# Three layers on one core: more places for the streamed weight blocks, the last attention pairs three steps apart, another order of issue

## The chip, the cores and the metric

One Trainium2 chip; the program runs on one of its cores. Five engines work side by side, each in its own order: PE (TensorE, matrix products; its weight loads stand apart as PEld), DVE (VectorE), ACT (ScalarE), POOL (GpSimd) and SP (SyncE, which here only issues DMAs). The metric is device microseconds of one execution; lower is better.

## The reference

Three parts follow each other. The second and third take their input from the part before them.

```python
# q, k, v: (4, 8, 576, 64) float32
out_d = softmax(mean4(q) @ mean4(k).T / 8) @ mean4(v)       # sequence pooled by 4
out   = repeat(out_d, 4) + softmax_near(q @ k.T / 8) @ v    # near: |i - j| < 4
x = out as (2304, 512)
h = x @ w_in;  g = max(h, 0) + log1p(exp(-abs(h)));  x = g @ w_out   # first layer, 512 -> 2048 -> 512
h = x @ w_in2; g = h * cos(h);                       y = g @ w_out2  # second layer, same sizes
```

The weights arrive as float64. The products are made of 16-bit pieces: each operand is split in a high and a low part, and three matmuls (high by high, high by low, low by high) stand for one.

## The kernel before

**Tiles and products.** The 2304 tokens are five tiles: 0 to 3 of 512 tokens, 4 of 256. L1 and L2 are the first layer's two products, L3 and L4 the second layer's. Attention is 16 pairs of heads (batch b, column c). L1 and L2 keep their weights in on-chip memory (`w1i_t`, `w1o_t`). L3 and L4 use schemes with seven products in place of eight, so their weights grow to seven quarters.

**Second weights.** A block of `w2i` or `w2o` is loaded as float64, decoded on ACT and DVE (`rebase`, `top`, `join`, `bound`, four `sums`, `high`, `low`: class `Second`), and stored to device memory (`scr_in`, `scr_out`). `second(n)` adds the decodes of n blocks to the program; it is called beside the first layer's units. The decode uses room that attention has had (`place2`); the room of the decode becomes the places of the last stage (`place3`).

**Streamed blocks.** L3 reads `scr_in` once for each of the five tiles: 40 loads of 896 KB into two places, `ri0` and `ri1`. L4 reads `scr_out`: 7 products by 2 halves by 5 tiles, 70 loads of 512 KB into four places, `ro0` to `ro3`. A place is refilled when the last matmul that reads it is done. For tile 4 such a block serves 12 matmuls of 256 columns, for a longer tile 24. All loads stand in SP's queue, one behind the other.

**Who sets the order.** The code adds operations to a plan (`Plan.add`) with a cost on each engine that may do them. `due()` works out backward when each has to be done; `move()` adds offsets from the table `MOVES`; `order()` runs a list schedule forward in which a place is taken when free. What comes out is the order of each engine's instructions, and it is held to (each engine's instructions are tied to the one before). Work that either ACT or DVE may do (casts `gh`, splits `high`, `xhi`) goes to the one that is free there. PE takes its matmuls in this order and passes none over.

**Steps.** `step()` counts first-layer units on their way into the plan: 28 are counted before tile 1's first unit, and each unit of a later tile counts two. Attention pair 4 and later ones are added at the steps in `POS1`, `POS2`, `POS3`. While attention has little for PE, matmuls on a tile of zeros (line 2089) are put in.

Names that the prediction uses: line 1386 is L1's matmul, 1623 L2's, 1430 L3's, 1722 L4's; 1681 takes L4's sums out of PSUM; 531 and 533 are one cast on ACT and on DVE, 525 and 527 one scaling; `xt0` to `xt4` hold the inputs of the tiles, in L1 and again in L3.

Of the kernel before, what the change touches and what calls it, by code (L numbers as in the profile page):

```python
# [27 lines left out]
NB = NF // 2  # L28
# [25 lines left out]
POS2 = (37, 41, 45, 49)  # L54
POS3 = (54, 58, 62, 66)
# [6 lines left out]
ONES, FROM, LONG = range(0, 10, 2), (4, 0), (2, 4)  # L62
# [9 lines left out]
W2STEP = 2  # L72
# [103 lines left out]
class Op:  # L176
    def __init__(self, n, cost, fn, claim, name, table=""):
        self.n, self.cost, self.fn, self.claim, self.name, self.table = n, cost, fn, claim, name, table
        self.succ, self.wait, self.values = set(), 0, set()
        self.hook, self.key = None, ""  # L180
# [1993 lines left out]
```

## Time and profile before

| | us |
|---|---|
| median of 3 runs | 857.46 |
| the runs | 855.68, 857.46, 859.52 |
| the profiled execution | 859.96 |
| its span, first to last instruction | 858.1 |
| busy: PE, DVE, ACT | 822.7, 734.8, 543.5 |

The stretches: to about 100 us attention and the decode of the first weights; to about 300 the rest of attention beside tiles 0 to 2 of the first layer; to 470 tiles 2 to 4 beside the decode of the second weights; from 470 L3 and L4, with L3 of one tile beside L4 of the tile before it; from about 823 L4 of the last tile alone.

A busy PE in this profile may still be late: its matmuls overlap, so the spacing of their ends tells their pace. A wait is idle time of an engine that something else ended.

### The profile page before, as it was taken

Reading aid. Unit: us, or ns where it says so; the run is one execution under the profiler, and the core shown is the slowest. Engines: PE = TensorE matmul, PEld = TensorE weight load, DVE = VectorE, ACT = ScalarE, POOL = GpSimd, SP = SyncE. Lnnn points to the kernel's source line nnn. Section 1 sums busy time; section 2 is a strip of 40 time slices with the busy share of each in tenths; the row PEclk is TensorE's granted clock in tenths of the full one; section 3 lists DMA queues with packets and bytes.
Section 4 is the critical chain, followed back from the end, with each engine's and each line's share of the span. In section 5 each row is a group of like instructions: output and inputs, shape, how many; then the busy total and the mean of one; then the engine's idle time right before and its main releaser. Section 6 shows DMA issues by size and latency. Waiting matters only on the chain.

```text
span 858.1 us, 16959 instructions
## 1 busy us (share of the span) xinstructions
PE 822.7 (96%) x6837; PEld 543.3 (63%) x6837; DVE 734.8 (86%) x1570; ACT 543.5 (63%) x924; POOL 1.8 (0%) x9
## 2 busy tenths in 40 slices
PE   7988999999999999989999999999999999999986
PEld 3643555445555644434456888888666788888875
DVE  6999999866579867699999899999999999997651
ACT  3569999532244579799998789664565555564320
POOL 0000000000000000000000000000000000000000
PEclk9999999999999999999999999999999999999999
DMA  9887421202210054356746633356546576578676
GB/s 298 281 282 260 173 98 61 75 1 61 95 45 17 2 190 148 136 226 231 233 163 214 245 100 116 130 171 235 196 155 222 172 244 212 192 232 280 227 239 227
DMA packets 49310, 147.73 MB, mean 172 GB/s; under 512 B 3857, under 2 KB 22929, under 8 KB 45137
## 3 DMA queue, kind: packets, MB, share of 16 engines
q1 hardware_dynamic: 49232, 146.67, 50.9%
q8 instruction: 53, 0.87, 0.4%
q14 instruction: 25, 0.20, 0.1%
HBM read 127.25 MB, written 19.40 MB: 171 GB/s over the span
## 4 chain that ended last, share of the span: by engine, by line
PE 75%; DMA 11%; ACT 9%; DVE 4%; issue 1%; SPq 0%; POOL 0%; POOLq 0%; ACTq 0%
PE any L1623 19%; PE h L1430 17%; PE any L1722 16%; PE h L1386 15%; DMA ro<-scr_out 4%; DMA ri<-scr_in 4%; DMA qk<-qk 1%; PE any L1131 1%; DMA stg<-w1i 1%; ACT w1i_t L696 1%; PE any L847 1%; PE any L1006 1%; ACT ta L1560 1%; ACT tb L1564 1%; ACT ta L1572 1%
## 5 line engine op out<-in xcount | busy, mean ns | idle before, releaser
L1386 PE MATMUL h<-xt,w1i_t 128*128 128x512 f16 (+1 forms) x888 | 181.4, 356 | 0.2 <-DVE g L1343 0.2
L1623 PE MATMUL any<-g,w1o_t 128*128 128x512 f16 (+1 forms) x792 | 162.0, 353 | 1.3 <-DVE g L521 1.3
L1430 PEld LDWEIGHTS <-ri 128*128 128x128 f16 x1392 | 135.6, 98 | 41.6 <-DMA ri<-scr_in 7.4
L1386 PEld LDWEIGHTS <-w1i_t 128*128 128x128 f16 x888 | 86.1, 98 | 84.5 <-issue 4.0
L1623 PEld LDWEIGHTS <-w1o_t 128*128 128x128 f16 x888 | 85.8, 98 | 80.2 <-issue 2.6
L1722 PE MATMUL any<-ro,w1o_t 128*128 128x256 f16 x744 | 107.8, 275 | 6.6 <-DMA ro<-scr_out 5.9
L1430 PE MATMUL h<-xt,ri 128*128 128x256 f16 (+1 forms) x720 | 109.5, 294 | 3.8 <-DMA ri<-scr_in 3.1
L1722 PE MATMUL any<-ro,w1i_t 128*128 128x256 f16 x768 | 108.1, 273 | 3.8 <-DVE g L1681 1.9
L1430 PE MATMUL h<-tx,ri 128*128 128x256 f16 (+1 forms) x672 | 91.4, 280 | 2.3 <-DMA ri<-scr_in 2.3
L1722 PEld LDWEIGHTS <-w1i_t 128*128 128x128 f16 x768 | 75.1, 98 | 15.6 <-issue 3.9
L1722 PEld LDWEIGHTS <-w1o_t 128*128 128x128 f16 x744 | 73.1, 99 | 18.1 <-issue 6.4
L1514 ACT ACTIVATE tc<-ta,halfpi 128x512 f32<-128x512 f32 (+1 forms) x80 | 53.4, 675 | 33.2 <-DVE ta L1509 23.3
L513 DVE TENSOR_TENSOR gf<-gf 128x256 f32<-128x256 f32 (+1 forms) x160 | 58.6, 391 | 0.1
L1504 ACT ACTIVATE ta<-hs,quarter,i 128x512 int32<-128x512 f32 x48 | 38.1, 808 | 25.0 <-DVE hs L513 24.1
L513 DVE TENSOR_TENSOR w1i_t<-gf,w1i_t 128x512 f16<-128x512 f32 (+2 forms) x91 | 46.6, 526 | 1.7 <-ACT w1i_t L531 1.4
L1681 DVE SCALAR_TENSOR_TENSOR g<-any,ik,g 128x512 f32<-128x512 f32 (+1 forms) x35 | 23.8, 693 | 27.6 <-PE any L1722 26.7
L513 DVE TENSOR_TENSOR hs<-h,hs 128x512 f32<-128x512 f32 (+1 forms) x72 | 42.8, 596 | 2.9 <-PE h L1430 2.5
L1504 ACT ACTIVATE ta<-h,quarter,i 128x512 int32<-128x512 f32 (+1 forms) x32 | 21.2, 665 | 34.2 <-PE h L1430 34.1
L513 DVE TENSOR_TENSOR w1o_t<-gf,w1o_t 128x512 f16<-128x512 f32 (+1 forms) x69 | 41.9, 629 | 0.0
L531 ACT ACTIVATE w1o_t<-gf 128x512 f16<-128x512 f32 (+1 forms) x62 | 34.2, 580 | 10.0 <-DVE gf L513 6.5
L531 ACT ACTIVATE w1i_t<-gf 128x512 f16<-128x512 f32 (+2 forms) x77 | 36.4, 499 | 5.4 <-PE any L1722 2.1
L1553 ACT ACTIVATE ta<-h,i 128x512 f32<-128x512 f32 (+1 forms) x32 | 20.1, 632 | 25.8 <-PE h L1386 25.6
(218 smaller groups left out, 1293.5 us busy)
## 6 DMA issues: line engine op xcount, KB each, us to landing
ri<-scr_in SPq DMA_DIRECT2D x40, 896.0 KB, 4.6
ro<-scr_out SPq DMA_DIRECT2D x70, 512.0 KB, 4.9
qk<-qk SPq DMA_DIRECT2D x16, 589.0 KB, 4.1
stg<-w1i SPq DMA_DIRECT2D x8, 1024.0 KB, 7.3
stg<-w1o SPq DMA_DIRECT2D x8, 1024.0 KB, 4.7
stg<-w2i SPq DMA_DIRECT2D x8, 1024.0 KB, 4.8
stg<-w2o SPq DMA_DIRECT2D x8, 1024.0 KB, 4.8
scr_in<-dec SPq DMA_DIRECT2D x8, 896.0 KB, 4.2
```

Of the source, the lines that this page charges most:

```text
L513: eng[e].tensor_tensor(out=out, in0=in0, in1=in1, op=op)
L531: nc.scalar.activation(out=out, in_=in_, func=AF.Copy)
L696: nc.scalar.activation(out=out().rearrange("p (m e) -> p m e", m=2), in_=self.floats(b), func=AF.Abs, accum_out=self.bd[:, b : b + 1],)
L847: nc.tensor.matmul(pa.t[64 * h : 64 * h + 64, j, 64 * g : 64 * g + 64], tk.t[64 * j : 64 * j + 64, 0, q0 + 3 : q0 + 67], tk.t[64 * j : 64 ...
L1386: nc.tensor.matmul(h.t[:, 0:n], l, r, start=(i == 0), stop=(i == 11))
L1430: nc.tensor.matmul(h.t[:, a : a + m], l, r, start=(i == 0), stop=(i == n - 1))
L1504: act(n, 2, psum), lambda: nc.scalar.activation(out=bits(a()), in_=x(), func=AF.Identity, scale=col(o.i2, f), bias=quarter), [*keys, *sc], ...
L1514: act(n, 1), lambda: nc.scalar.activation(out=r(), in_=a(), func=AF.Sin, scale=TWOPI, bias=halfpi),
L1553: act(n, 1, True), lambda: nc.scalar.activation(out=x(), in_=h.t[:, 0:n], func=AF.Softplus, scale=col(o.i1, f)),
L1623: nc.tensor.matmul(a.t[:, i, 0:n], l, r, start=(first and j == 0), stop=(last and j == 2))
L1681: dve(256 * m, False, 1), lambda: nc.vector.scalar_tensor_tensor(out=o.t[:, 0 : 256 * m], in0=view(k), scalar=T[t].ik, in1=x.t[:, 0 : 256 ...
L1722: nc.tensor.matmul(a.t[:, z, 256 * c : 256 * c + 256], l, r, start=(b == 0 and x == 0), stop=(b == NB - 1 and x == 2),)
```

## The change

1. **Places.** `xt0`, the input of tile 0, becomes a third place for L3's blocks once tile 0's L3 matmuls are done. `xt1`, `xt2` and `xt3` become two places each for L4's blocks, once their tile's L3 matmuls are done: four places become ten. `spare` puts them on the lists.
2. **A later landing in the plan.** The streamed loads get `lag = STREAM`, 2.0 us by which the plan takes them to land later, in `due()` and in `order()`.
3. **Attention's last eight pairs** are added at every third step (steps 37 to 58), not every fourth (37 to 66).
4. **Decode of the second weights**: one block at each unit of tile 2 and on (`W2STEP` 1), not one at every second unit; with 3. the first is added at tile 2's unit 0, not unit 3.
5. **Offsets**: the table `MOVES` is another one, some 330 numbers. All of them go into the order.

```diff
-POS2 = (37, 41, 45, 49)
-POS3 = (54, 58, 62, 66)
+POS2 = (37, 40, 43, 46)
+POS3 = (49, 52, 55, 58)
-ONES, FROM, LONG = range(0, 10, 2), (4, 0), (2, 4)
+ONES, FROM, LONG, STREAM = range(0, 10, 2), (4, 0), (2, 4), 2.0
-W2STEP = 2
+W2STEP = 1
...
-    "L1 0 0": -800, "L1 0 1": 102, "L1 0 1 mm#1": -108, "L1 0 10 relu#1": 41.5, "L1 0 11": 13, "L1 0 12 mm#1": -24.5,
+    "L1 0 0": -520, "L1 0 0 G#1": 491, "L1 0 1": -37.5, "L1 0 10 mm#1": 26.5, "L1 0 11": 14.5, "L1 0 11 G#1": -23.5,
...
-                end[q] = min(end[q], op.due - LAT[min(q.cost, key=lambda z: q.cost[z])])
+                end[q] = min(end[q], op.due - LAT[min(q.cost, key=lambda z: q.cost[z])] - q.lag)
...
-                heapq.heappush(done, (end + LAT[op.eng], -1 - n, op))
+                heapq.heappush(done, (end + LAT[op.eng] + op.lag, -1 - n, op))
...
+            flat = [xt16[t].rearrange("p c n -> p (c n)") for t in range(4)]
+            RI.tiles.append(flat[0][:, 0:3584].rearrange("p (h e) -> p h e", h=2))
+            for x in flat[1:]:
+                for a in (0, 2048):
+                    RO.tiles.append(x[:, a : a + 2048].rearrange("p (b h e) -> p b h e", b=4, h=2))
...
+        def spare(t):
+            done = [o for o in P.ops if o.name.startswith(f"L3 {t} ") and "pe" in o.cost]
+            def add():
+                if t:
+                    RO.free.extend([NRO + 2 * t - 2, NRO + 2 * t - 1])
+                else:
+                    RI.free.append(NRI)
+            P.add({"pool": 0.01}, lambda: None, [], [], [], "dead", after=done).hook = add
```

**PE, around the first matmul of L3.** Rows are line, instruction, output and inputs, size. Before:

```order
L1623 LDWEIGHTS w1o_t_162
L1623 MATMUL any0_87<-g7_110,w1o_t_162 128x256
L1623 LDWEIGHTS w1o_t_162
L1623 MATMUL any0_87<-g7_110,w1o_t_162 128x256
L1430 LDWEIGHTS ri0_4420
L1430 MATMUL h3_3135<-xt0_82,ri0_4420 128x256
```

After (lines of the new file are 2 higher):

```order
L1388 LDWEIGHTS w1i_t_161
L1388 MATMUL h1_773<-xt4_86,w1i_t_161 128x256
L1388 LDWEIGHTS w1i_t_161
L1388 MATMUL h1_773<-xt4_86,w1i_t_161 128x256
L1432 LDWEIGHTS ri0_4264
L1432 MATMUL h3_3112<-xt0_82,ri0_4264 128x256
```

L3 now begins among tile 4's L1 matmuls, with 756 of L1's 888 and 690 of L2's 888 matmuls ahead of it, where 804 and 744 stood ahead before; the matmuls on zeros ahead of it are 75, were 83.

**SP, the loads around the start of tile 1's L3.** `ri` and `xt0` are places for L3's blocks, `ro` for L4's. Before:

```order
L1436 DMA ri0_4420<-scr_in0_250 128x3584
L1436 DMA ri1_4421<-scr_in1_251 128x3584
L1436 DMA ri0_4420<-scr_in2_252 128x3584
L1436 DMA ri1_4421<-scr_in3_253 128x3584
L1436 DMA ri0_4420<-scr_in4_254 128x3584
L1709 DMA ro0_4422<-scr_out_258 128x2048
L1709 DMA ro2_4424<-scr_out_258 128x2048
L1709 DMA ro1_4423<-scr_out_258 128x2048
L1709 DMA ro3_4425<-scr_out_258 128x2048
```

After:

```order
L1438 DMA ri0_4264<-scr_in0_250 128x3584
L1438 DMA ri1_4265<-scr_in1_251 128x3584
L1438 DMA xt0_82<-scr_in2_252 128x3584
L1438 DMA ri0_4264<-scr_in3_253 128x3584
L1438 DMA ri1_4265<-scr_in4_254 128x3584
L1711 DMA ro2_4268<-scr_out_258 128x2048
L1711 DMA ro0_4266<-scr_out_258 128x2048
L1438 DMA xt0_82<-scr_in5_255 128x3584
L1711 DMA ro1_4267<-scr_out_258 128x2048
```

The third block of tile 1 goes into `xt0` and no longer waits for `ri0` to come free. In the whole program L3 reads 312 of its 1392 matmuls' blocks from `xt0`, and L4 600 of 1512 from `xt1` to `xt3`.

**SP, the last loads of L4.** `out` are results on their way to device memory. Before:

```order
L1709 DMA ro2_4424<-scr_out_258 128x2048
L1709 DMA ro0_4422<-scr_out_258 128x2048
L1709 DMA ro1_4423<-scr_out_258 128x2048
L1709 DMA ro2_4424<-scr_out_258 128x2048
L1709 DMA ro3_4425<-scr_out_258 128x2048
L1709 DMA ro0_4422<-scr_out_258 128x2048
L1709 DMA ro1_4423<-scr_out_258 128x2048
L1709 DMA ro2_4424<-scr_out_258 128x2048
L1709 DMA ro3_4425<-scr_out_258 128x2048
L1709 DMA ro0_4422<-scr_out_258 128x2048
L1709 DMA ro1_4423<-scr_out_258 128x2048
L1709 DMA ro2_4424<-scr_out_258 128x2048
```

After:

```order
L1711 DMA xt2_84<-scr_out_258 128x2048
L1711 DMA ro0_4266<-scr_out_258 128x2048
L1669 DMA out<-g5_108 128x2x256
L1711 DMA xt3_85<-scr_out_258 128x2048
L1669 DMA out<-g7_110 128x2x256
L1711 DMA xt1_83<-scr_out_258 128x2048
L1711 DMA ro2_4268<-scr_out_258 128x2048
L1711 DMA ro0_4266<-scr_out_258 128x2048
L1669 DMA out<-g6_109 128x2x256
L1711 DMA ro3_4269<-scr_out_258 128x2048
L1711 DMA xt2_84<-scr_out_258 128x2048
L1711 DMA xt3_85<-scr_out_258 128x2048
```

Four places took turns in these eleven loads; after, nine loads go to seven of the ten places (`xt1` to `xt3` hold two each), and three `out` stand among them.

## Rows read from the trace of the kernel before

**Rows 1.** Page, parts 1 and 2: busy time of the engines; the span in 40 slices
```profile
PE 822.7 (96%) x6837; PEld 543.3 (63%) x6837; DVE 734.8 (86%) x1570; ACT 543.5 (63%) x924; POOL 1.8 (0%) x9
...
PE   7988999999999999989999999999999999999986
```

**Rows 2.** Windows: length, busy us (x) of PE, PEld, DVE, ACT, POOL; PEclk, DMA share, GB/s
```profile
0.00:100.00 100.00, 87.78 (x918) 46.98 (x919) 89.27 (x173) 67.71 (x143) 1.77 (x9) 0.98 0.79 267
160.00:360.00 200.00, 200.00 (x1705) 103.07 (x1704) 146.97 (x337) 103.89 (x177) 0.00 (x0) 1.00 0.21 73
360.00:470.00 110.00, 106.87 (x583) 56.11 (x582) 107.82 (x223) 104.06 (x127) 0.00 (x0) 1.00 0.62 211
470.00:790.00 320.00, 309.93 (x2634) 256.65 (x2632) 307.27 (x645) 199.51 (x349) 0.00 (x0) 1.00 0.58 195
790.00:858.10 68.10, 58.35 (x507) 49.76 (x505) 29.08 (x85) 14.86 (x36) 0.00 (x0) 0.97 0.70 227
```

**Rows 3.** Waits of PE, whole span: us in total, times, longest us
```profile
PE any L1722 <- DMA ro<-scr_out: 7.3, 8, 1.7
PE h L1430 <- DMA ri<-scr_in: 5.4, 6, 2.1
...
PE any L1722 <- DVE g L1681: 2.4, 3, 1.3
...
PE h L551 <- ACT stg L1887: 1.8, 1, 1.8
...
PE any L1623 <- DVE g L521: 1.3, 1, 1.3
```

**Rows 4.** Waits of PE, 800 to 858.1 us
```profile
PE any L1722 <- DMA ro<-scr_out: 5.7, 6, 1.7
```

**Rows 5.** Loads of the first matmul blocks (tile ri), from issue to landing
```profile
DMA to landing us min/median/max: 4.4/4.6/7.3
```

**Rows 6.** Loads of the second matmul blocks (tile ro), from issue to landing
```profile
DMA to landing us min/median/max: 3.3/4.9/8.0
```

**Rows 7.** Chain of waits in order of time: start us, us, what, x pieces
```profile
174.44 10.36 PE h L1386 x48
...
471.07 9.34 PE h L1430 x84
...
549.27 5.24 PE h L1430 x48
...
808.62 8.84 PE any L1722 x81
```

**Rows 8.** Timeline of SP, 275 to 475 us: start us, us, queue, line, what
```profile
300.58 34.66 SPq L1861 DMA_DIRECT2D stg<-w2i  x6
...
466.28 1.58 SPq L1436 DMA_DIRECT2D ri<-scr_in  x2
```

**Rows 9.** Windows of 4 and 5 us, columns as in Rows 2
```profile
474.00:478.00 4.00, 4.00 (x39) 3.59 (x38) 3.11 (x7) 2.24 (x6) 0.00 (x0) 1.00 0.99 368
835.00:840.00 5.00, 3.30 (x20) 2.38 (x21) 0.48 (x1) 0.00 (x0) 0.00 (x0) 0.77 0.78 278
840.00:845.00 5.00, 4.51 (x36) 3.67 (x35) 0.45 (x1) 0.00 (x0) 0.00 (x0) 0.89 0.77 225
```

**Rows 10.** Groups of DVE by form: line, what, count, busy us, mean ns, idle before
```profile
L527 DVE TENSOR_SCALAR dec<-dec,s_w2i 128x1792 f16<-128x1792 f32 x4 | 4.6, 1150 | 0.0
...
L533 DVE CAST w1i_t<-gf 128x256 f16<-128x256 f32 x10 | 2.7, 285 | 0.0
...
L533 DVE CAST w1o_t<-gf 128x512 f16<-128x512 f32 x4 | 1.7, 420 | 0.0
```

**Rows 11.** Groups of ACT by form, table loads
```profile
L1553 ACT ACT_TABLE_LOAD x22 | 28.2, 1283 | 0.6 <-PE h L1386 0.2
```

**Rows 12.** Groups of PE by form, the matmuls that only keep PE busy
```profile
L2089 PE MATMUL any<-zero 128*128 128x512 f16 x83 | 22.8, 400 | 3.9 <-POOL zero L2078 2.1 <-DVE sm L513 1.4 <-ACT aTd L531 0.4
```

More of the change, by code (lines that the diff above doesn't have):

```diff
@@ L179, in __init__ @@
         self.succ, self.wait, self.values = set(), 0, set()
-        self.hook, self.key = None, ""
+        self.hook, self.key, self.lag = None, "", 0.0
 class Plan:
@@ L389, in order @@
                     for e in s.at:
-                        s.at[e] = max(s.at[e], op.end + LAT[op.eng])
+                        s.at[e] = max(s.at[e], op.end + LAT[op.eng] + op.lag)
                     s.wait -= 1
@@ L1436, in block_in @@
                 dma(917), lambda: nc.sync.dma_start(w.t, scr_in[b]), [("scr", "w2i", b), "place3"], [w], [w], f"L3 {t} {2 * b} load"
-            )
+            ).lag = STREAM
             return w
@@ L1710, in l4 @@
                         [("scr", "w2o", b) for b in range(NB)] + ["place3"], [w], [w], f"L4 {t} {j} load",
-                    )
+                    ).lag = STREAM
                 for c in range(m):
@@ L2030, in free_slots @@
             P.add({"pool": 0.01}, lambda: None, [], [], [], "dead", after=ops).hook = add
-        used = {(W, b): [] for W in (W1I, W1O) for b in range(NB)}
+        def spare(t):
[6 more added lines that the diff above has]
+            P.add({"pool": 0.01}, lambda: None, [], [], [], "dead", after=done).hook = add
         for i, (k, t, f) in enumerate(seq):
@@ L2049, in build @@
                 pair_in(0, b)
+                if b == NB - 1:
+                    spare(0)
         drain(0)
@@ L2061, in build @@
         )
-        pair_ops = None
         for t in range(4):
@@ L2072, in build @@
                 pass
+            if t < 3:
+                spare(t + 1)
         for _ in l4(4):
```

138 rows, old and new, of the table MOVES are left out of this document.

## The prediction

> **What bounds the kernel now.** I read the page first: PE is busy 822.7 of 858.1 us [rows 1], so PE sets the end, and only three things can move it: its idle time, the zero matmuls, a lower clock. Its work stays what it is, since the changed order holds the same matmuls but for eight zero ones. The 40 slices [rows 1] show it in the first four, in the 18th and in the last two. The windows say what is short in each stretch [rows 2]: to 100 us PE idles 12.2 us; from 160 to 360 nothing; from 360 to 470 it idles 3.1 us while DVE is busy 98% of the time; from 470 to 790 it idles 10.1 us, DVE 12.7; from 790 on 9.8 us, with DVE free. Then the waits of PE by releaser [rows 3]: 7.3 us for L4's blocks (eight times), 5.4 us for L3's (six times), 2.4 us for the engine that empties L4's sums, 1.8 and 1.3 us for the decode and DVE in the stretch from 360 to 470. Of the 7.3 us, 5.7 fall after 800 us [rows 4].
>
> Why PE waits for blocks follows from a count along the order. For each refill of a place I add up the matmuls between the last that reads the old block and the first that reads the new one; with 48 matmuls of 256 columns in 5.24 us and 81 in 8.84 [rows 7] one is 0.109 us, and 48 of 512 columns in 10.36 us make 0.216. This gap is the time that a refill has. A refill lands 4.6 us (L3) and 4.9 us (L4) after its issue in the middle, 3.3 at the least and 8.0 at the most [rows 5, 6]. Before, 31 of 104 refills have under 4.9 us; the shortest of L3's have 5.2, and of the 14 blocks of the last tile 13 have 2.9 to 4.2 us. Those must stall. After, none of 97 refills has under 5.9 us (SP's queue order taken in, so a load behind a waiting load counts from that one's release: on SP the next loads and the results stand behind each waiting load, and PE waits for the loads); the middle one has 13.7, was 6.2; of the last tile's 14 the shortest has 6.2.
>
> **The change part by part**, against the profiled execution's own 859.96 us.
>
> *Last tile's blocks.* The waits of 5.7 us [rows 4] go. Six of the last 14 blocks are released 20 us or more before they are needed, so the DMA has them in before PE comes. −5.7.
>
> *Waits for blocks before that.* 7.3 − 5.7 = 1.6 us for L4's and 5.4 us for L3's [rows 3]; the third place serves L3 from tile 1 on, and in tile 0, still with two, the new order leaves 7.8 us or more where 5.9 and 5.2 stood. −7.0. What stands next in the queue behind them is DVE's work, below.
>
> *The clock.* In the last stretch the granted clock is 0.77 in 835 to 840 us and 0.89 in 840 to 845, after PE's waits there; elsewhere it is 1.00 [rows 9, 2]. That is the lower of the two levels, 1.2 GHz, for part of these stretches; the work lost is 0.23 × 5 + 0.11 × 5 = 1.7 us. Without the waits I take it back. −1.7.
>
> *DVE.* The new order moves work from ACT to DVE: casts to 16 bits go from 28 to 47 on DVE, at 0.29 to 0.42 us [rows 10], and splits of 1792 columns from 8 to 11, at 1.15 us: some 19 × 0.34 + 3 × 1.15 = 9.9 us. From 470 to 790 DVE is busy 307.3 of 320 us [rows 2], so with the waits for blocks gone it comes close to PE. Against it: L3 starts earlier, and so does DVE's part of it. Ahead of L3's first matmul stand 48 L1 matmuls of 256 columns, 48 L2 ones of 256, 6 of 512 and eight zero ones fewer: 96 × 0.109 + 6 × 0.216 + 8 × 0.27 = 13.9 us (a zero one is 22.8 / 83 = 0.27 us [rows 12]). That work now stands beside L3, where DVE wants the time; and from 160 to 360 DVE has 53 us idle [rows 2], into which the earlier decode moves. Bounds: 0, if the 13.9 us cover it, and +9.9 if nothing does. I take 3.0, nearer to the covered end. +3.0.
>
> *L3's first matmul.* PE passes nothing over, so if the first block isn't there it stands. The decode now needs to be done 13.9 us earlier. Attention's last matmul has 12 L1 matmuls of 512 columns and eight zero ones fewer ahead of it, 4.8 us; the rest must come out of the chain from the first load of second weights to the first load of L3, 300.58 to 466.28 us, 165.7 us [rows 8]. One block per unit in place of one per two speaks for it: from 160 to 360 DVE and ACT have room [rows 2]. Bounds: 0, and 13.9 − 4.8 = 9.1 us if the chain is as long as before. I take 0.
>
> *Attention closer together.* Eight pairs in 24 steps, not 32; PE idles nowhere from 160 to 360 and DVE is busy 147 of 200 us [rows 2], so the cover is there. If it went, the same work on DVE would hold PE: bounds ±2.2 us, the eight zero matmuls, which stand only where PE has nothing else. I take 0. The first 100 us, where DVE is busy 89%, get another order of the same work; taken as 0, inside the same bounds.
>
> *The waits for the decode and DVE*, 1.8 + 1.3 + 2.4 us [rows 3]: I leave them in. Bounds −5.5 and 0.
>
> Sum: 859.96 − 5.7 − 7.0 − 1.7 + 3.0 = 848.6 us. The profiled execution was 2.5 us above the median of 857.46, so 846.1: **846 us**.
>
> One rule of the Trainium skill speaks against the change. The trace: a 512 KB block lands 3.3 us after issue at the least, 4.9 in the middle, 8.0 at the most [rows 6], and DMA carries 195 to 227 GB/s in this part [rows 2]. The Trainium skill, "DMA: Bandwidth & Descriptors", section "Latency and other measured facts", gives the access to device memory as 0.2 us on average and 2 us under high load: more loads in flight would each come later. By it the middle landing would be 4.9 + 1.8 = 6.7 us; 8 of 97 refills have less, 5.2 us in all, and the sum would be 846 + 5 = 851 us. The spread from 3.3 to 8.0 us agrees with it; whether more places bring more of it, no row of before shows.
>
> **Rivals.**
>
> *A. DVE takes PE's waits over.* For it: 307.3 busy of 320 us, and 9.9 us more work. Against it: the earlier start, and DVE's last work on L3 being done before about 823 us with PE still having the last tile. Then the 7.0 us of block waits turn into waits for DVE and half of the 9.9 us adds to them: 859.96 − 5.7 − 1.7 + 5 − 2.5 = 855 us.
>
> *B. Slower: L3's first matmul stands.* For it: the chain of 165.7 us has to shrink by 9.1, and inside it come three more table loads on ACT (51, were 48, at 1.28 us [rows 11]) and at worst all 9.9 us of DVE's new work. Against it: the room from 160 to 360. The stand would be 9.1 + 3.8 + 9.9 = 22.8 us: 859.96 − 14.4 + 22.8 − 2.5 = 866 us. It decides the sign from a stand of 14.4 + 4.3 = 18.7 us on.
>
> *C. Loads crowd each other.* DMA reached 368 GB/s for 4 us [rows 9], so the wires carry more than the 227 of the last stretch. But if landings come to 8.0 us, 17 refills fall short by 19.9 us in all; half of that, since one stall gives the next load time: 859.96 − 14.4 + 10 − 2.5 = 853 us. The rule of the Trainium skill above is the page's word for it; its 851 us lie inside this case.
>
> *D. All small waits go too.* DVE costs nothing and the 5.5 us of the decode and DVE vanish with the earlier decode: 859.96 − 14.4 − 5.5 − 2.5 = 838 us.
>
> That the places go unused is excluded by the order: 312 of L3's and 600 of L4's matmuls read from them.
>
> **How the numbers follow.** Forecast 0.58, its own range 841 to 851; A 0.14, B 0.06, C 0.10, D 0.12. The range 838 to 856 holds the forecast, D and most of A and C. A measurement here tells 0.5% from no change: 853.2 and 861.7 us. Faster: 0.58 + 0.12 + half of C and 0.04 of A = 0.79; slower: B, 0.06; the same: the rest, 0.15.
>
> **What would show it.** Right: the waits of PE for L4's blocks after 800 us under 1 us, where 5.7 stood, and the granted clock 1.00 there; waits for L3's blocks under 1.5 us in all; L3's first matmul at about 457 us, 14 before 471.07 [rows 7]; PE's idle time from 470 to 790 under 5 us. A shows as waits of PE for DVE (lines 1681, 531, 513) of more than 7 us; B as one wait of 9 us or more before L3's first matmul; C as landings with a middle above 6 us. The forecast is wrong if PE's waits for blocks fall by less than 8 of their 12.7 us, or if waits on DVE and ACT grow by more than 8.

## The result and the profile after

The changed kernel takes 835.43 us (median of 4 runs, 834.93 to 838.67), the kernel before 856.92 us beside it: ratio 0.9753, 95% interval 0.9719 to 0.9787, 21.5 us faster. A second set (e13_after) gave 834.67 us and 0.9730 (0.9704 to 0.9756). The forecast was 846 us with a range of 838 to 856: the direction was right, the gain nearly twice what was forecast (21.5 for 11.4 us), and the time lies below the range.

Parts 1 and 2 of the page of the kernel after (busy time of the engines; PE in 40 slices):

```profile
PE 817.8 (98%) x6829; PEld 543.0 (65%) x6829; DVE 744.2 (89%) x1594; ACT 536.5 (64%) x903; POOL 1.8 (0%) x9
...
PE   8998999999999999999999999999999999999997
```

The span is 833.7 us, was 858.1: 24.4 less, of which PE's busy time gives 4.9 and its idle time 19.5. The lower digit in the middle of [rows 1] and one of the two at the end are gone; the first 100 us still have lower digits.

The windows of the kernel after say where the idle time went (columns as in [rows 2]):

```profile
0.00:100.00 100.00, 90.59 (x927) 47.91 (x927) 88.31 (x174) 68.74 (x144) 1.78 (x9) 0.98 0.72 244
160.00:360.00 200.00, 200.00 (x1707) 103.41 (x1705) 159.98 (x353) 109.23 (x189) 0.00 (x0) 1.00 0.26 92
360.00:470.00 110.00, 108.59 (x616) 59.70 (x615) 107.34 (x219) 97.61 (x124) 0.00 (x0) 1.00 0.65 221
470.00:790.00 320.00, 319.10 (x2731) 266.80 (x2729) 307.74 (x660) 197.85 (x337) 0.00 (x0) 1.00 0.59 202
790.00:833.70 43.70, 39.50 (x359) 34.86 (x357) 23.07 (x70) 10.92 (x26) 0.00 (x0) 0.98 0.58 190
```

Against [rows 2], PE's idle time falls from 12.2 to 9.4 us up to 100 us, from 3.1 to 1.4 in 360 to 470, from 10.1 to 0.9 in 470 to 790, and from 9.8 to 4.2 after 790. DVE's busy time rises by 13.0 us between 160 and 360, and by 0.5 between 470 and 790. These windows stand on the clock, and the kernel after is 17.4 us ahead at L3's first matmul, so equal windows hold unequal work there. Windows that go with the work, from L3's first matmul to its last, before and after:

```profile
471.07:822.40 351.33, 341.87 (x2924) 285.27 (x2925) 325.15 (x698) 209.53 (x373) 0.00 (x0) 1.00 0.59 198
453.63:806.90 353.27, 352.37 (x3035) 296.61 (x3034) 336.49 (x736) 221.49 (x379) 0.00 (x0) 1.00 0.59 203
```

Beside L3 DVE has 11.3 us more to do, and PE's idle time falls from 9.5 to 0.9 us all the same.

All waits of PE after 100 us that the view lists (us in total, times, longest):

```profile
PE h L1388 <- ACT ta L1555: 1.4, 1, 1.4
PE any L1724 <- ACT g L527: 1.1, 3, 0.4
PE any L1724 <- DVE g L1683: 0.2, 1, 0.2
```

The 12.7 us for blocks [rows 3] are gone to the last one, and most of the 5.5 us for the decode and DVE too.

The last stretch in windows; its granted clock stood at 0.77 and 0.89 in two windows of before [rows 9]:

```profile
815.00:825.00 10.00, 10.00 (x94) 8.97 (x92) 2.59 (x5) 0.00 (x0) 0.00 (x0) 1.00 0.75 252
825.00:830.00 5.00, 4.73 (x42) 3.85 (x40) 0.79 (x2) 0.00 (x0) 0.00 (x0) 1.00 0.15 52
```

The timeline of SP (first load of second weights, first load of L3) and the chain of waits (L3's first matmul):

```profile
294.85 16.43 SPq L1868 DMA_DIRECT2D stg<-w2i  x4
...
446.47 0.84 SPq L1438 DMA_DIRECT2D ri<-scr_in  x2
```

```profile
453.63 9.17 PE h L1432 x84
```

From the one load to the other it is now 151.6 us, was 165.7 [rows 8]; L3 begins 17.4 us earlier than in [rows 7], where 14 were forecast.

### The profile page after: what moved, and what is told of

Its sections match the earlier page's. It is cut to its first block, busy times and chain, and to the rows that moved or that the text cites. A ratio compares the mean times of both kernels' runs of the same rounds, so it can differ in the third digit from the quotient of the medians.

```text
span 833.7 us, 16948 instructions
## 1 busy us (share of the span) xinstructions
PE 817.8 (98%) x6829; PEld 543.0 (65%) x6829; DVE 744.2 (89%) x1594; ACT 536.5 (64%) x903; POOL 1.8 (0%) x9
## 4 chain that ended last, share of the span: by engine, by line
PE 84%; DVE 6%; DMA 5%; ACT 3%; issue 1%; POOL 0%; POOLq 0%; SPq 0%; ACTq 0%
PE h L1432 21%; PE any L1724 20%; PE any L1625 19%; PE h L1388 18%; PE any L1361 2%; DMA vd<-vd 2%; DMA stg<-w1i 2%; PE any L1133 1%; DVE w1i_t L676 1%; DMA stg<-w1o 1%; PE any L1008 1%; DVE dec L523 1%; PE any L849 1%; DMA vw<-vw 1%; DMA stg<-w2o 1%
## 5 line engine op out<-in xcount | busy, mean ns | idle before, releaser
L1432 PEld LDWEIGHTS <-ri 128*128 128x128 f16 x1080 | 105.7, 98 | 22.9
L1724 PEld LDWEIGHTS <-w1i_t 128*128 128x128 f16 x756 | 73.9, 98 | 11.3 <-issue 1.0
L1432 PE MATMUL h<-xt,ri 128*128 128x256 f16 (+1 forms) x540 | 80.5, 290 | 0.0
L1432 PE MATMUL h<-tx,ri 128*128 128x256 f16 (+1 forms) x540 | 72.3, 278 | 0.0
L1724 PE MATMUL any<-ro,w1i_t 128*128 128x256 f16 x477 | 71.3, 273 | 0.7 <-ACT g L527 0.7
L1724 PE MATMUL any<-ro,w1o_t 128*128 128x256 f16 x435 | 65.6, 273 | 0.2 <-DVE g L1683 0.2
L1724 PE MATMUL any<-xt,w1o_t 128*128 128x256 f16 x321 | 49.7, 273 | 0.4 <-ACT g L527 0.4
L515 DVE TENSOR_TENSOR w1i_t<-gf,w1i_t 128x256 f16<-128x256 f32 (+2 forms) x90 | 46.5, 523 | 0.2
L1724 PE MATMUL any<-xt,w1i_t 128*128 128x256 f16 x279 | 43.4, 273 | 0.0
L1432 PEld LDWEIGHTS <-xt 128*128 128x128 f16 x312 | 30.5, 98 | 10.1
```

The source lines that it names most:

```text
L515: eng[e].tensor_tensor(out=out, in0=in0, in1=in1, op=op)
L1432: nc.tensor.matmul(h.t[:, a : a + m], l, r, start=(i == 0), stop=(i == n - 1))
L1724: nc.tensor.matmul(a.t[:, z, 256 * c : 256 * c + 256], l, r, start=(b == 0 and x == 0), stop=(b == NB - 1 and x == 2),)
```

## The experiments

The kernel before ran beside each of them, at 857 to 859 us. Kernels of one chip are compared by their medians (e1 to e4; e5 to e8; e9 to e12; e13 to e16), others by their ratios times 857 us. Where a kernel has DVE work added, that work is not the reference's.

**Places alone, in the old order.** These four keep the order of PE, DVE and ACT of the kernel before, word for word. After the plan is made, the streamed loads are taken out of it and issued anew as soon as a place is free; the inputs of finished tiles become places when their last L3 matmul stands. The four differ in two numbers.

```diff
+            RI.tiles.append(flat[0][:, 0:3584]...)      # and xt1 to xt3 as places for L4's blocks
-        ops, all4 = P.order(), list(BANK.tiles)
+        ops, all4 = reissue(P.order(), 2, 4), list(BANK.tiles)   # e1: 2, 4  e2: 3, 4  e3: 2, 10  e4: 3, 10
```

e1_reissue, the control. 

> The kernel before, with the order of PE, DVE and ACT kept word for word and the loads of streamed blocks put into SP's queue anew, each as early as a place is free: still two places for L3's and four for L4's blocks. It is the control of the next three. Theory P (the gain is in the places): 23 of 104 refills have under 4.9 us, were 30, so nearly nothing changes, 852 to 857 us. Theory O (the gain is in the new order; the places are worth little, since DVE takes over): 855 to 858 us.

859.43 us, ratio 1.0010 (0.9979 to 1.0041): issuing anew changes nothing that can be told from noise, and both theories had set it some us too low.

e2_third_ri, the third place for L3. 

> As e1, and tile 0's input is a third place for L3's blocks; L4's keep four. Theory P: the waits for L3's blocks (5.4 us in 6 waits of the kernel before) fall to under 2 us, and each wait that goes gives back some 0.3 us more than the idle time shown, since the first matmul after a wait starts a new run: 5 to 7 us below e1, about 848 us. Theory O: within 3 us of e1, the waits for blocks turned into waits for DVE.

853.87 us, 0.9958 (0.9933 to 0.9982): 5.6 us under the control, as places should bring. The 0.3 us per wait is measured by no run here: in the trace a matmul of 256 columns takes 273 ns and neighbours end 109 ns apart, which makes 0.16 us for the first behind a wait.

e3_ro10, ten places for L4. 

> As e1, with ten places for L4's blocks (the inputs of tiles 1 to 3 hold two each) and two for L3's. Theory P: of the waits for L4's blocks (7.3 us in 8 waits) nearly all go, the granted clock after 835 us is 1.00, and the last stretch shortens: 9 to 12 us below e1, about 845 us. Theory O: the last tile alone gains, 4 to 7 us, and waits for DVE grow before it.

849.67 us, 0.9899 (0.9866 to 0.9931): 9.8 us under the control.

e4_both, all places. 

> As e1, with the third place for L3's blocks and ten for L4's: the places of the change on the old order of PE, DVE and ACT. Theory P: both gains add up, 16 to 19 us below the kernel before, 838 to 841 us, most of the change's 21.5 us. Theory O: not below 848 us; the rest of the change's gain needs the new order.

843.09 us, 0.9829 (0.9789 to 0.9869): 14.7 us below before and 16.3 below the control, from places alone. Waits of PE, first of e1_reissue, then of e2_third_ri, of e3_ro10 and of e4_both:

```profile
PE any L1722 <- DMA ro<-scr_out: 6.2, 11, 1.2
PE h L1430 <- DMA ri<-scr_in: 6.0, 8, 1.9
```

```profile
PE any L1722 <- DMA ro<-scr_out: 8.7, 10, 1.7
...
PE h L1430 <- DMA ri<-scr_in: 1.5, 3, 0.8
```

```profile
PE h L1430 <- DMA ri<-scr_in: 2.9, 5, 1.1
```

```profile
PE any L1722 <- DVE g L1681: 2.6, 4, 1.3
PE h L551 <- ACT stg L1892: 1.8, 1, 1.8
PE any L1623 <- DVE g L521: 1.3, 1, 1.3
...
PE h L1430 <- DMA ri<-scr_in: 0.3, 1, 0.3
```

Each set of places takes away most or all of the waits for its own blocks. They touch the other's too: the ten places for L4 halve the waits for L3's blocks (2.9 us, 6.0 in the control), and the third place for L3 leaves more for L4's (8.7, was 6.2). With both, 0.3 us is left of 12.7, and the waits for the decode and DVE of [rows 3] stand as before. So theory P has it, though its 838 to 841 us were 2 us too low, and the last 6.5 to 8.5 us of the gain (0.9829 against 0.9753 and 0.9730) come from the other order.

**The new order, one part undone or done alone.**

The order is made anew in these, except in e6_ri2. No run undoes the table of offsets or the later landing (changes 5 and 2) alone.

e5_w2step: the kernel after with the decode at every second unit again.

```diff
-W2STEP = 1
+W2STEP = 2
```

> The kernel after with one number put back: the second weights are decoded one block at every second unit of tile 2 and on. The first 2320 matmuls of PE are the same as in the kernel after; L3's first matmul stands 11.8 us of PE work later (535.8 us of matmuls ahead of it, 524.0 in the kernel after), one refill has 1.0 us less than the 4.9 of a middle landing, the matmuls on zeros are the same 75. Theory E (the part of the gain that the places don't explain, some 8 us, comes from the earlier decode: it frees DVE later and takes away the small waits): 839 to 843 us, PE's waits for ACT and DVE after 300 us at 4 us or more, where the kernel after has 2.8. Theory F (that part comes from the other order of the first 160 us, which this kernel keeps): 834 to 837 us, waits as in the kernel after.

866.95 us, 1.0102 (1.0086 to 1.0119): 30 us above the kernel after. Theory E has the sign, but four times its size; F falls. One window and the worst wait, 470 to 790 us, of e5_w2step; under it the same window of the kernel after:

```profile
460.00:490.00 30.00, 29.30 (x261) 25.23 (x259) 7.56 (x16) 18.31 (x31) 0.00 (x0) 1.00 0.52 194
...
PE h L1432 <- DVE hs L515: 6.3, 6, 3.4
```

```profile
460.00:490.00 30.00, 30.00 (x271) 26.32 (x270) 29.57 (x66) 29.76 (x47) 0.00 (x0) 1.00 0.34 120
```

DVE idles 22 of these 30 us, where the kernel after has it full (29.57 us): L3, whose sums DVE makes, begins at 467.5 us, not at 453.6, and PE still has matmuls of the first layer to do, which give DVE little. From 490 us on PE waits for DVE. What DVE doesn't do there it doesn't get back.

e10_pos_back: the kernel after with attention's last eight pairs four steps apart.

```diff
-POS2 = (37, 40, 43, 46)
-POS3 = (49, 52, 55, 58)
+POS2 = (37, 41, 45, 49)
+POS3 = (54, 58, 62, 66)
```

> The kernel after with the positions of attention's last eight pairs put back to four steps apart; the decode still one block per unit. The first 1136 matmuls of PE are the same; 81 matmuls on zeros in place of 75 (1.6 us), L3's first matmul behind 530.6 us of matmuls, 524.0 in the kernel after, one refill 0.3 us short. Theory C (closer pairs are what brings DVE's work in before 360 us): DVE busy 147 to 154 us between 160 and 360, waits for DVE and ACT after 360 us of 8 us or more, 845 to 860 us. Rival N (the decode's spacing alone does it): DVE busy 158 us or more there, 836 to 839 us.

865.73 us, 1.0074 (1.0043 to 1.0104): 28 us above the kernel after; theory C, over its range. SP's timeline, two windows, and two waits of e10_pos_back:

```profile
323.13 17.85 SPq L1868 DMA_DIRECT2D stg<-w2i  x4
```

```profile
160.00:360.00 200.00, 200.00 (x1705) 103.18 (x1704) 141.68 (x323) 89.89 (x168) 0.00 (x0) 1.00 0.18 62
360.00:470.00 110.00, 92.09 (x422) 41.22 (x420) 106.80 (x195) 92.46 (x102) 0.00 (x0) 0.92 0.58 206
```

```profile
PE h L1388 <- DVE xt L1297: 10.9, 2, 8.8
PE h L553 <- ACT stg L1894: 5.0, 2, 4.0
```

The decode takes attention's room, so its first load waits for attention's end: 323.13 us, was 294.85. DVE's work between 160 and 360 falls to 141.68 us, and what is missing there makes PE stand in the next stretch, where DVE is full. So the closer pairs are what brings DVE's work to where it has time.

e11_w2_old: e4_both with the decode at every unit; PE's order doesn't change.

```diff
-W2STEP = 2
+W2STEP = 1
```

> The kernel before with all ten and three places (as in e4_both, order of before) and one more number changed: the decode one block at every unit. PE's order is that of the kernel before, word for word; ACT and DVE take the decode in another order. Theory E (the earlier decode by itself takes the small waits away): waits of 1.8 and 1.3 us between 360 and 400 gone, 838 to 841 us. Rival N (it needs the rest of the new order, since PE's order doesn't follow): 842 to 845 us, as e4_both.

854.91 us, 0.9950 (0.9928 to 0.9972): 10 us above e4_both; neither theory. A wait of PE, and one of ACT between 360 and 390 us:

```profile
PE h L1386 <- ACT ta L1553: 11.5, 1, 11.5
```

```profile
ACT stg L1892 <- DVE dec L1884: 5.0, 3, 2.0
```

In ACT's queue rounds of the decode, which wait for DVE three times, now stand ahead of the operation that PE's L1 needs; PE stands for 11.5 us at 373. So the denser decode alone costs; it gains only with the rest.

e6_ri2: the kernel after with two places for L3.

```diff
-        ops, all4 = P.order(), list(BANK.tiles)
+        ops, all4 = reissue(P.order(), 2, 10), list(BANK.tiles)
```

> The kernel after with two places for L3's blocks in place of three; L4 keeps ten; the order on PE, DVE and ACT is untouched, the loads are issued as soon as a place is free. Counted along the order, 7 refills have less than the 4.9 us of a middle landing, by 13.4 us in all. Theory P (each refill that is short makes PE stand by what is short): 847 to 851 us, PE's waits for L3's blocks 12 to 15 us in 7 waits. Rival Q (one stall gives the next load its time, as the prediction took it for its case C: half): 840 to 844 us, 5 to 8 us of waits. Rival R (the third place is worth nothing in the new order): 834 to 837 us.

861.91 us, 1.0033 (1.0009 to 1.0057): 24 us above the kernel after, more than any theory. Its waits of PE after 100 us, and the windows of the first long one and just behind it:

```profile
PE h L1432 <- DMA ri<-scr_in: 13.3, 6, 3.1
PE h L1432 <- DVE gf L515: 2.4, 1, 2.4
PE h L1432 <- DVE sg L512: 1.5, 1, 1.5
```

```profile
559.00:564.00 5.00, 1.88 (x17) 1.40 (x16) 2.45 (x6) 0.98 (x3) 0.00 (x0) 0.97 0.51 187
564.00:569.00 5.00, 5.00 (x33) 3.88 (x32) 3.78 (x8) 3.73 (x7) 0.00 (x0) 0.68 0.00 0
```

The waits for blocks are what was counted: 13.3 us, counted 13.4. But they cost nearly twice that (the span is 24.4 us longer). PE's busy time is 824.0 us, 6.2 more than in the kernel after. In part that is the granted clock, which falls at three of the five long waits (0.68 in 564 to 569 us behind one of 3.1 us, so part of the time at the lower of the two levels, 1.2 and 2.4 GHz; 0.72 and 0.83 in the 5 us that hold two of 2.8 and 2.4 us) and stays at 1.00 at two others (2.8 and 1.9 us). PE's waits for DVE, 3.9 us, are probably late work that the waits for blocks passed on; that isn't shown. In the old order the same place was worth 6.6 us (e3_ro10 against e4_both), here 24: the new order counts on three places.

**DVE's price.** The kernel after with additions of 128x256 on DVE, 28 or 59 after L3's first matmul, or 34 from tile 1's L1 to tile 3's L1 (178 to 368 us in the trace of e14_dve_mid).

```diff
+            if late and o.eng == "dve" and o.name[:4] != "L4 4":     # mid: from L1 of tile 1 to L1 of tile 3
+                count += 1
+                if count % 27 == 0:                                   # e8: 13, mid: 10
+                    x = Op(-1, {"dve": 0.4}, lambda: two("dve", pad, pad, pad, ALU.add), (), "pad")
```

e7_dve12. 

> The kernel after with 28 more additions of 128x256 on DVE, spread evenly over its work from L3's first matmul to the last tile; at 0.417 us each (the same form in the kernel after) 11.7 us. It adds work that the reference doesn't need. DVE idles 12.3 of 320 us between 470 and 790 us. Theory S (what DVE has in idle time takes it up; the prediction's 3.0 us for 9.9 us of DVE work was not there): 835 to 837 us. Rival T (DVE is as good as the bound in this stretch, as the prediction's case A has it: half or more of it shows): 841 to 847 us. The prediction's own rate, 3.0 for 9.9: 839 us.

838.27 us, 0.9767 (0.9751 to 0.9783), near the prediction's own rate.

e8_dve25. 

> The same with 59 additions, 24.6 us, twice what DVE idles there. Theory S: up to the idle time nothing shows, beyond it every us does: 24.6 - 12.3 = 12.3 us, 846 to 850 us. Rival T (it shows from the first us on): 856 to 860 us. Rival U (DVE works ahead of PE in the buffers that it has, and the work it has after L3's end takes up the rest): 835 to 840 us.

845.08 us, 0.9832 (0.9809 to 0.9855): between U and S. Its runs spread from 840.65 to 846.23 us.

e9_dve_mid. 

> The kernel after with 34 more additions of 128x256 on DVE, 14.2 us by 0.417 each, spread over its work between about 170 and 355 us. It adds work that the reference doesn't need. The kernel after has 13.0 us more DVE work between 160 and 360 us than the kernel before (159.98, was 146.97), and DVE still idles 40 us there. Theory S (the prediction's DVE term was booked in the wrong stretch: work that lies here is free): within 1 us of the kernel after, 834 to 837. Rival T (it costs what the same additions cost after 470 us, 0.24 us per us): 838 to 840.

837.27 us, 0.9735 (0.9706 to 0.9765). The intervals of e7_dve12 and e9_dve_mid overlap that of the kernel after too much for a term of 3 us, so the next four ran on one chip.

e13_after. 

> The kernel after once more, as the measure for the three runs beside it on the same chip: 833 to 838 us.

834.67 us, 0.9730 (0.9704 to 0.9756).

e14_dve_mid. 

> The kernel of e9_dve_mid again (34 more additions on DVE between 170 and 355 us, 14.2 us). Theory S (free there): within 1.5 us of e13_after. Rival T (same price as after 470 us): 3 to 4 us above it.

836.18 us, 0.9757 (0.9730 to 0.9785): 1.5 us more, inside the intervals; it lies on the bound of S and is half of what T asks. A wait of PE in 360 to 380 us, in e14_dve_mid and in e9_dve_mid alike and not in the kernel after, says where 1 us of it goes:

```profile
PE h L1388 <- DVE xt L1297: 1.2, 1, 1.2
```

e15_dve12. 

> The kernel of e7_dve12 again (28 more additions on DVE after L3's first matmul, 11.7 us). Theory R (the prediction's rate was right, 3.0 for 9.9): 2.0 to 4.5 us above e13_after. Rival Z (free here as well): within 1.5 us of it.

837.94 us, 0.9772 (0.9748 to 0.9796): 3.3 us more, theory R.

Windows of e14_dve_mid, of e15_dve12 and of e8_dve25:

```profile
160.00:360.00 200.00, 199.97 (x1706) 103.44 (x1705) 168.19 (x383) 108.17 (x187) 0.00 (x0) 1.00 0.25 90
```

```profile
470.00:790.00 320.00, 317.26 (x2705) 264.29 (x2704) 311.37 (x677) 198.13 (x336) 0.00 (x0) 1.00 0.58 197
```

```profile
470.00:790.00 320.00, 312.36 (x2650) 258.80 (x2648) 313.53 (x686) 193.03 (x326) 0.00 (x0) 1.00 0.57 193
```

Before 360 us, 8 us more on DVE leave PE at 199.97 of 200 us; just behind, PE's idle time from 360 to 470 us grows from 1.2 (e13_after) to 2.2 us. So it is cheap there and not quite free. After 470, the doses take PE from 319.10 to 317.26 and 312.36, with DVE not yet full: its work costs from early on there, and more with the dose (3.3 us for the first by e15_dve12, 6.8 more by the medians for the second, e8_dve25 against e7_dve12). What the two runs in the middle measure is the room before 360 us. They don't bear on the prediction's DVE term: its casts stand beside L3 (next section).

**Loads as early as can be.** e12_early_loads and e16_early_loads: the kernel after with its loads issued as soon as a place is free.

```diff
+        ops, all4 = reissue(P.order(), 3, 10), list(BANK.tiles)
```

> The kernel after with its streamed loads issued as soon as a place is free, in the order of their first readers; PE, DVE and ACT as they are. No refill has under 5.9 us either way, the middle one 15.4 us in place of 13.7. Theory S (no load is late, so earlier ones bring nothing): 834 to 837 us, no wait of PE for a block. Rival C (more loads in flight crowd each other and come after PE): landings of L4's blocks with a middle above 6 us and waits for them, 838 us or more.

833.68 us, 0.9700 (0.9672 to 0.9728).

> The kernel of e12_early_loads again (loads as soon as a place is free). Theory S (no load is late in the kernel after): within 1.5 us of e13_after. Rival L (some loads still come late by what the profile doesn't show as a wait): 1.5 to 4 us below it.

834.69 us, 0.9737 (0.9711 to 0.9762), 0.02 us from e13_after. The gap of the first run isn't there on one chip: no load is late in the kernel after, and no kernel here is shown to be faster than it.

## Why the prediction was wrong, step by step

**The step that failed** is the price of the other order. The places were priced at −14.4 us with the clock; e4_both, which has them and nothing else, measured −14.7 (−11 to −18). All the rest was priced at +3.0: the DVE term at +3.0, the small waits at 0, the first 100 us at 0. It measured −7.7 (from e4_both's 843.09 to 835.43 us; −6.5 to −8.5 by the ratios). The terms one by one:

**Last tile's blocks, and those before it** (−5.7 and −7.0): right. All 12.7 us went.

**The clock** (−1.7): right in size for the execution that was profiled, but not shown to belong to the waits. It is 1.00 where 0.77 and 0.89 stood. In e1_reissue, where PE still waits 4.5 us for L4's blocks after 800 us, the same two windows have it at 1.00:

```profile
835.00:840.00 5.00, 3.26 (x29) 2.53 (x28) 0.07 (x1) 0.00 (x0) 0.00 (x0) 1.00 0.90 304
840.00:845.00 5.00, 4.26 (x38) 3.42 (x36) 0.67 (x2) 0.00 (x0) 0.00 (x0) 1.00 0.86 286
```

So the low clock may be part of why that execution stood 2.5 us above the median, and the sum then takes it off twice. Nor was the clock 1.00 in all other stretches: it is 0.98 up to 100 us [rows 2], as in the kernel after.

**DVE** (+3.0): the place was right for most of the work, the cost did not come. DVE's casts for L4's operands, before and after (count, shortest, middle and longest in ns, first and last start):

```profile
L533 DVE CAST w1i_t<-gf x14: 220/286/421, 528.7 to 826.5; 128x256 f16<-128x256 f32 x10, 128x512 f16<-128x512 f32 x3, 128x128 f16<-128x128 f32 x1
L533 DVE CAST w1o_t<-gf x7: 283/419/422, 551.5 to 813.2; 128x512 f16<-128x512 f32 x4, 128x256 f16<-128x256 f32 x3
L535 DVE CAST w1i_t<-gf x24: 215/286/421, 469.3 to 811.1; 128x256 f16<-128x256 f32 x13, 128x512 f16<-128x512 f32 x6, 128x128 f16<-128x128 f32 x5
L535 DVE CAST w1o_t<-gf x16: 282/419/427, 469.5 to 811.3; 128x512 f16<-128x512 f32 x10, 128x256 f16<-128x256 f32 x6
```

The 19 more, some 6.3 us by the trace, all stand behind L3's first matmul, where they were booked (the three splits of 1792 columns belong to the decode and stand before it), and DVE is fuller there (336.5 of 353.3 us, was 325.2 of 351.3). Yet PE's waits for the engine that empties L4's sums fell from 2.4 to 0.2 us. It came out at the lower bound, 0. The +13.0 us between 160 and 360 us are other work: 9.2 of them are the decode, which came forward (operations on tile `dec`: 31.0 us there, were 21.8). Why the casts cost nothing stays open. Additions put into the finished order in that stretch do cost, at the rate that was forecast (e15_dve12: 3.3 us for 28). The casts, unlike them, were in the plan, which gives such work to the engine that is free; no run has the new order with the old casts.

**The waits for the decode and DVE** (0, bounds −5.5 and 0): mis-sized, most of them went. With two smaller ones they were 6.6 us in the kernel before and are 2.7 now: −3.9. The places alone leave them (e4_both), and so it is the other order that took them.

**L3's first matmul** (0, up to 9.1): right, it doesn't stand; the chain from the first load of second weights shrank by 14.1 us, and began 5.7 us earlier.

**Attention closer together, and the first 100 us** (0 ± 2.2): mis-sized. PE's idle time up to 160 us fell by 3.1 us. It isn't chance alone: the twelve kernels here that keep this front (the first 1136 matmuls or more) have PE busy for 89.6 to 91.4 of the first 100 us, 90.4 on average, the six with the old one for 86.3 to 89.9, 88.0 on average. Which number of the table does it stays open. For the pairs the bound of ±2.2 was far too narrow: taken back alone, they cost 28 us (e10_pos_back). They were priced as if nothing depended on them but their own cover; in fact the decode waits for attention's room.

The sum: forecast −11.4 from the profiled 859.96; the steps missed 3.0 (DVE), 3.9 (small waits) and 3.1 (front). Of PE's busy time, down 4.9, the clock explains 1.7; 3.2 more fell, spread over several lines (1.3 us in L2's matmuls, 0.9 in L1's, 0.6 in the zero ones). Part of that is one execution against another: e1_reissue, with the order and the waits of before, has 820.3 us, and one kernel has 818.7 in e9_dve_mid and 820.4 in e14_dve_mid. Why the rest fell stays open. That makes 13.2 of the 13.1 us between the sum of 848.6 and the profiled 835.5 us.

**The rivals.** D, which had all small waits go and DVE cost nothing, came nearest (838 us, given 0.12); it lacked the front (the first 160 us). A fell: waits for DVE after 470 us went from 2.4 to 0.2 us. B fell: no stand before L3's first matmul. C fell; the landings of the kernel after, L3's blocks and then L4's in their own places:

```profile
DMA to landing us min/median/max: 4.5/4.7/7.5
```

```profile
DMA to landing us min/median/max: 4.6/5.5/6.4
```

The middle rose by 0.1 us and by 0.6 against [rows 5, 6], the longest fell for L4's, and no load came after PE; loads into `xt0` to `xt3` land in 4.8 us in the middle and 7.0 at the most. C's sign, a middle above 6 us, does stand in e4_both, without C's price; L3's blocks there, in their own places, for which PE waits 0.3 us:

```profile
DMA to landing us min/median/max: 4.3/6.1/8.4
```

The rule of the Trainium skill ("DMA: Bandwidth & Descriptors", section "Latency and other measured facts") agrees here at most in direction: 0.6 us more for L4's blocks, and 1.5 for L3's in e4_both, where its 0.2 to 2 us would have made 1.8. Whether the access to device memory is what takes longer, no run shows. In the kernel after, with refills of 5.9 us and up, even that was covered.

**The method.** The time was forecast as the sum of edits priced one by one. For the places this holds, within the interval. For the order it doesn't: the closer pairs, the denser decode and the offsets together gain 6.5 to 8.5 us; the first taken back costs 28, the second taken back 30, and the second alone, on the old order, 10. The range was built from bounds of single edits and ended at D.

## What to carry to other kernels

Count the gap of each refill along the order and compare it with the landing time: on the new order that gave the waits to within a microsecond (13.4 counted, 13.3 measured in e6_ri2), though their cost with what follows was nearly twice that. Where more work lands on a nearly full engine, look first in which stretch, by its idle time there: the same kind of work cost 3 us in one stretch and 1.5 or less in another, and planned work cost nothing that shows even in the first. When a change moves the program in time, compare stretches that hold the same work, not the same times of the clock. Edits that only work together (when one thing ends, when the next begins, and the offsets made for both) are one edit with one wide bound, and undoing one of them measures their dependence, not its share.

## What was not expected of the hardware

A wait of PE costs more than it shows: in e6_ri2 18.2 us more idle time came with 6.2 us more busy time for the same matmuls, with the clock at 0.68 in the 5 us behind a wait of 3.1, though not behind each long wait. And an instruction more on DVE costs less than its duration: 34 additions of 0.415 us each, 14.1 in all, raised DVE's busy time from 744.2 to 753.8 us (e9_dve_mid), 0.28 each, so neighbours overlap for a third of it.
